# A new hand-written order between the folds of a Fourier layer and the first output tiles of the MLP behind it

## The chip, the cores and the metric

The kernel runs on one core of a Trainium2 chip. A core has a matrix engine (PE in the profile), a vector engine (DVE), a scalar engine (ACT), a general engine (POOL) and a queue that issues most of the transfers (SP). Each engine works through its own instructions in order and waits for the others by semaphores. PE writes only to PSUM, a memory of eight banks, from which DVE and ACT read; POOL works on the main on-chip memory (SBUF) alone. The metric is the time of one execution in microseconds (us), lower is better.

## The reference, cut to what matters

Three layers follow one another on two sequences (b = 0, 1) of 768 tokens with 512 features:

```python
attn = retention(q, k, v, lam)                       # blocks of tokens with a running state
X = np.real(np.fft.fft(np.fft.fft(x, axis=1), axis=2))   # over tokens, then over features
u = x + X
un = (u - mean(u)) / sqrt(var(u) + 1e-6)
u = u + maximum(un @ w_ch1, 0) @ w_ch2               # first MLP, 512 -> 2048 -> 512
xn = (u - mean(u)) / sqrt(var(u) + 1e-6) * g_ln
out = u + maximum(xn @ w_ch1b, 0) @ w_ch2b           # second MLP
```

All of it is computed to nearly float32 accuracy: in the MLPs a float32 operand is split into two 16-bit parts, `hi` and `lo`, and a product is three matmul passes (hi by hi, hi by lo, lo by hi).

## The kernel before

The tokens are handled as twelve tiles of 128: for each sequence three tiles `U[b][0..2]` and three mirrored ones `U[b][3..5]`, since the transform over the tokens is done by its symmetry. MLP work runs in blocks of three tiles (384 tokens); there are four blocks, two a sequence.

Up to the first MLP block everything is a chain for b = 0: retention; the folds (`fold_half`, lines 483 to 499), in which DVE adds and subtracts a tile and its mirror and then folds over the features; the first transform over the tokens (`dft1_part`, `dft1_out`: five groups g of matmuls over three folds m, then ACT copies each group out of PSUM); the second transform over the features, a sine half (`dft2_q`: PE, then two ACT copies into `qs`; `sub_sin`: it is applied to `u` in two additions) and a cosine half (`dft2_p` on PE, `add_cos` on DVE); the norm (`ln_steps`: DVE statistics, two small DVE steps, a power on POOL; `ln_pe_steps`: a small DVE step and the scaling `un` on ACT, four transposes on PE, the copy of the hi part on ACT, the subtraction for the lo part on DVE); and the first output tiles of the MLP (`part`, `mlp_part`: 12 matmuls for one tile of tokens j and one of 16 slices f of the hidden layer). The program does this for f = 0, 1, 2 only, nine parts in all.

Meanwhile weights are converted. `conv_steps` (line 283) makes the two 16-bit halves of a 128x512 weight piece in four steps: ACT expands the upper bits into one of three buffers `top`; DVE shifts the lower bits and combines both (two instructions, lines 294 and 295); ACT rounds to the hi half (308); POOL subtracts for the lo half (310). With `which=None` DVE keeps its middle result in SBUF, with a name of banks ("at", "up") in PSUM. Pieces (1,0,0) to (1,0,3), the first quarter of the first weight matrix, are needed before the first part of the MLP; (2,0,0) and (2,0,1) are the first pieces of the second matrix, and the next quarter of the first is (1,0,4) to (1,0,7).

The order of the stretch is written by hand in the string `ORDER` (line 44). Each word runs the next step of a chain: `k`/`j` are the cosine and sine half of a fold, `d24` the matmuls of fold 2 for group 4, `D3` the copy of group 3, `c0` to `c3` the conversions, `R` the fold of one extra row (ACT then POOL), `q X p P` the second transform of a tile, `b n` the norm, `W27` 27 matmuls whose result is not used, `M12` the part of the MLP for tile 1 and slice 2. PE, DVE, POOL and ACT take these instructions in the order of the string, word by word. In the string of before the steps of the three tiles are mixed; so are the conversions, whose last steps stand among the second transforms:

```python
    chains[f"c{i}"] = lambda i=i: conv_steps(1, 0, i, None if i else "at")
```

Behind the string a planner orders the rest by its own estimate of times: for each step n of the MLP the matmuls up and down and the tasks of a table `bg` (weight conversions, the retention of b = 1, norms). `after(i, task)` (line 973) sets the instructions of a task on one engine behind a gate. The gates are the last POOL power of `ln_steps` ("pool") and the last lo subtraction of `ln_pe_steps` on DVE ("dve"). The mirrored tiles are finished by `dft2_y0` on POOL, behind the gate "pool", and `dft2_y`; conversions (2,0,0) and (2,0,1) stand behind "dve".

Of the kernel before, what the change touches and what calls it, by code (L numbers as in the profile page):

```python
# [15 lines left out]
ALU = mybir.AluOpType  # L16
# [4 lines left out]
B, H, S, D = 2, 8, 768, 64  # L21
# [7 lines left out]
ND = DM // 2 + 1  # L29
# [12 lines left out]
YS = 2.0 ** -15  # L42

ORDER = """
c0 S B1 B0 s s B1 B0 s s O4 B1 B0 O4 c0 I O4 R I O5 O5 O5 O5 c0 c1 c2 W12 k2 j2 k2 k2 d24 d20 d21 j2 j2 d22 d23
k1 k1 k1 d14 d10 d11 j1 j1 j1 d12 d13 c3 j0 j0 j0 d03 k0 k0 k0 d02 c1 D3 R c2 R c0 D2 d04 d01 D4 d00 c3 D1 q0 D0 q0
c1 q2 q2 X0 X0 q1 q1 c2 X1 p0 p1 P0 c1 X1 P1 b0 b1 b0 X2 c3 p2 c2 b0 b1 X2 P2 c3 b0 n0 b1 b2 b1
W27 n0 b2 n1 n0 b2 W6 n1 n0 b2 M00 n2 n1 n2 n2 n1 M01 M12 M11 M10 n2 M22 M20 M02 M21
"""
ONPOOL = "Y1 Y2"  # L50
LD1 = ()
# [1 line left out]
EARLY0, GATEN, B1, SPC, DS, DC, DFO, DD, D1S, D2S, AO, YA, NR, NE, LN1, L1, L2, F01, F02, TL, R1, R2, SE, PR1, LAG, UB, FB, NW, MQ, SPL = 11, 8, 3, 2.0, 2.0, 5, 1.0, 0.5, 0.5, 1.0, "aba", "aa", 2, 0, 2, 2.5, 2.5, 16, 4, 3, 1.5, 2, "dddd_dppp", 0, 3, 3, 13, 11, 1, 3  # L53
# [71 lines left out]
def tile_retention_fourier_mlp(ctx: ExitStack, tc: tile.TileContext, a: dict, out: bass.AP):  # L125
    nc = tc.nc
    pe, act, dve, pool, sp = nc.tensor, nc.scalar, nc.vector, nc.gpsimd, nc.sync
# [18 lines left out]
    def bank(which, name):  # L146
        return banks[which].tile([P, 512], F32, tag=which, name=name)
# [103 lines left out]
    def w_load(kind, m, i, room=None):  # L251
        t = room
        if t is None:
            t = wst.tile([P, 512, 2], I32, tag="ws", name=f"ws{kind}_{m}_{i}")
        staged[kind, m, i] = t
        return sp.dma_start(t.rearrange("p n two -> p (n two)").bitcast(I16)[:, :2047], w_src(kind, m, i).bitcast(I16)[:, 1:2048])
# [6 lines left out]
    def run(steps):  # L263
        for t in steps:
            pass
        return t

    def w_conv(kind, m, i):
        return run(conv_steps(kind, m, i, "at"))
# [13 lines left out]
    def conv_steps(kind, m, i, which=None, into=None):  # L283
        if (kind, m, i) not in staged:
            w_load(kind, m, i)
        raw = staged.pop((kind, m, i))
        top = tops[n_top[0] % 3]
        n_top[0] += 1
        t = wtp.tile([P, 512], F32, tag="wt", name=f"wf{kind}_{m}_{i}")
        ti = t.bitcast(I32)  # L290
        part = ti if which is None else bank(which, f"ps_w{kind}_{m}_{i}").bitcast(I32)
        act.activation(top[:, :, 1], raw.bitcast(BF16)[:, :, 2], AF.Copy, scale=TOPS)  # L292
        yield t
        dve.tensor_scalar(part, raw[:, :, 0], 13, None, op0=ALU.logical_shift_right)  # L294
        dve.tensor_tensor(ti, part, top.rearrange("p n two -> p (n two)").bitcast(I32), op=ALU.bitwise_or)  # L295
        yield t
        if kind == 1:
            g, k = divmod(i, 4)
            if (m, g) not in w1t:
                w1t[m, g] = wpool.tile([P, 2, 4, 512], F16, tag=f"w1_{g}", name=f"w1_{m}_{g}")  # L300
            hi, lo = w1t[m, g][:, 0, k], w1t[m, g][:, 1, k]
        else:
            if into is None:
                into = w2t[m, i] = wpool.tile([P, 2, 512], F16, tag=f"w2_{i}", name=f"w2_{m}_{i}")
            hi, lo = into[:, 0], into[:, 1]
        if kind == 1 and m == 1:
            act.activation(t, t, AF.Copy, scale=gcol[:, k:k + 1])
        act.copy(hi, t)  # L308
        yield t
        (dve if m == 0 and i in (LD1 if kind == 1 else LD2) else pool).tensor_tensor(lo, t, hi, op=ALU.subtract)  # L310
        yield t
# [134 lines left out]
    def attn_s_steps(b, c, bk):  # L446
        new, old = states[c % 2], states[(c - 1) % 2]
        if c > 0:
            dec = stp.tile([P, H // 2 * D], F32, tag="dec", name=f"dec{b}_{c}")
            do, di = (z.rearrange("p (i d) -> p i d", d=D) for z in (dec, old))  # L450
            pool.tensor_tensor(do, di, lc.unsqueeze(2).to_broadcast([P, H // 2, D]), op=ALU.mult)
        yield
        k_ = ks[b, c]
        ps = bank(bk["st"], f"ps_st{b}_{c}")
        for h in range(H):
            (i, e), hc = divmod(h, 2), slice(h * D, (h + 1) * D)
            for n, (x, y) in enumerate(PASS):
                pe.matmul(ps[e * D:(e + 1) * D, i * D:(i + 1) * D], k_[:, x, hc], vs[b, c][:, y, hc],
                          start=n == 0, stop=n == 2)
        yield  # L460
        psv = ps[:, :H // 2 * D]
        if c == 0:
            dve.tensor_copy(new, psv)
        else:
            dve.tensor_tensor(new, psv, dec, op=ALU.add)
        yield
        if b == 0:
            for e in range(2):
                r = slice(e * D, (e + 1) * D)
                act.copy(diag[c % 2][r, :, e * D:(e + 1) * D], new[r].rearrange("p (i d) -> p i d", d=D))  # L470
        yield
# [110 lines left out]

    def sub_sin(b, j, eng=pool):
        qs, x_ = qst[j], U[b][j]
        dve.tensor_tensor(x_[:, :ND], x_[:, :ND], qs, op=ALU.subtract)
        yield
        eng.tensor_tensor(x_[:, ND:], x_[:, ND:], qs[:, 255:0:-1], op=ALU.add)
        yield
# [14 lines left out]
    def dft2_y0(b, j):  # L603
        qs, y_ = qst[j], U[b][3 + j]
        pool.tensor_tensor(y_[:, :ND], y_[:, :ND], qs, op=ALU.add)
        pool.tensor_tensor(y_[:, ND:], y_[:, ND:], qs[:, 255:0:-1], op=ALU.subtract)
# [30 lines left out]
    unT, unt, gate = {}, {}, {}  # L637
# [19 lines left out]
    def ln_n(m, blk, j):  # L657
        u = U[blk // 2][(blk % 2) * 3 + j]
        mv, rs = unt.pop((m, blk, j))
        un = unt[m, blk, j] = f32t(f"un{m}_{blk}_{j}")  # L660
        dve.scalar_tensor_tensor(rs[:, 0:1], mv[:, 0:1], -1.0, rs[:, 1:2], op0=ALU.mult, op1=ALU.mult)
        act.activation(un, u, AF.Identity, bias=rs[:, 0:1], scale=rs[:, 1:2])
# [12 lines left out]
    def ln_pe_steps(m, blk, j, bk):  # L675
        if (m, blk) not in unT:
            unT[m, blk] = untp.tile([P, 2, NK, TB], F16, tag="unT", name=f"unT{m}_{blk}")
        ln_n(m, blk, j)
        yield
        un, t = unt.pop((m, blk, j)), unT[m, blk][:, :, :, j * P:(j + 1) * P]  # L680
        ps = bank(bk["l"], f"ps_l{m}_{blk}_{j}")
        for k in range(NK):
            pe.transpose(ps[:, k * P:(k + 1) * P], un[:, k * P:(k + 1) * P], ident)
        yield
        psv = ps.rearrange("p (k t) -> p k t", k=NK)
        act.copy(t[:, 0], psv)
        yield
        gate["dve"] = dve.tensor_tensor(t[:, 1], psv, t[:, 0], op=ALU.subtract)
        yield
# [238 lines left out]
    def eng(n):  # L928
# [3 lines left out]
    chains = {"s": lambda: attn_s_steps(0, 4, bk0), "O4": lambda: attn_o_steps(0, 4, bk0),  # L932
              "O5": lambda: attn_o_steps(0, 5, bk0), "I": lambda: attn_i_steps(0, 5, bk0), "R": lambda: row_fold(0)}
# [5 lines left out]
    for g in range(5):  # L939
        chains[f"D{g}"] = lambda g=g: dft1_out(0, g, ps1[g])  # L940
    for i in range(NE, 4):
        chains[f"c{i}"] = lambda i=i: conv_steps(1, 0, i, None if i else "at")
    for j in range(3):
        chains[f"q{j}"] = lambda j=j: dft2_q(0, j, bk0)
        chains[f"X{j}"] = lambda j=j: sub_sin(0, j, eng(f"Y{j}"))
        chains[f"b{j}"] = lambda j=j: ln_steps(0, 0, j)
        chains[f"n{j}"] = lambda j=j: ln_pe_steps(0, 0, j, bk0)
# [25 lines left out]
    def after(i, task):  # L973
        with tc.issue_after(gates[i]):
            task()

    gates = {x: g.ins for x, g in gate.items()}
    for j in range(3):
        after("pool", lambda: dft2_y0(0, j))
    after("dve", lambda: [w_conv(2, 0, i) for i in range(2)])  # L980
    for j in range(3):
        dft2_y(0, j, bk0) if YA[0] == "a" else after("dve", lambda: dft2_y(0, j, bk0))

# [21 lines left out]
    for c in range(NCH):  # L1005
        t = B1 + SPC * c
# [3 lines left out]
    n = t + DC + DFO  # L1010
# [25 lines left out]
    n0 = (NB - 1) * NF  # L1036
# [16 lines left out]
    def step(n):  # L1053
        m = n // (NB * NF)
        return m, order[m][n // NF % NB], n % NF
# [3 lines left out]
    for (m, blk), f in fast_from.items():  # L1059
        for kk in range(2):  # L1060
            if m == 0 and blk < 3:
                put(16 * blk + f / 2 + kk - 3, lambda blk=blk, kk=kk: un_sums(0, blk, kk))
            else:
                at = m * NB * NF + order[m].index(blk) * NF
# [4 lines left out]
    for n in range(total + LAG):  # L1069
        rest = None  # L1070
        if n < total:
            m, blk, f = step(n)
            if n >= SPL:
                rest = (mlp_up if f < fast_from.get((m, blk), NF) else mlp_up_fast)(m, blk, f)
        for _, _, task in sorted(bg.pop(n, ()), key=lambda z: z[0]):
            after("dve", task) if n < GATEN else task()
        if n >= LAG:
            mlp_down(*step(n - LAG))
        if rest:
            rest()  # L1080
# [26 lines left out]
```

## Time and profile before

| | us |
|---|---|
| three runs, median (lowest, highest) | 605.07 (604.65, 605.29) |
| the profiled execution | 605.77 |
| its span in the trace | 603.9 |
| last fold on DVE ends | 48.37 |
| last of the nine MLP parts ends | 71.6 |

Times inside the trace are counted from the start of the span. A view that lists instructions merges neighbours of one kind on one engine (x12 is twelve of them) and shows in brackets how long the engine stood idle before them and whose end released it. PE's matmuls overlap one another, so the length of one is more than the step from one to the next.

### The profile page before, as it was taken

The page shows a single profiled execution, that of the slowest core. Times are in us where ns is not written, and L with a number is a line of the kernel's source. Part 1 is how long each engine was busy: PE and PEld are TensorE (multiplying, and loading weights), DVE is VectorE, ACT ScalarE, POOL GpSimd, SP SyncE. Part 2 cuts the span into 40 slices and gives each one's busy share as a digit, 9 for nine tenths or more (in the row PEclk, how much of TensorE's full clock was granted, in tenths as well). Part 3 has the DMA queues.
Part 4 walks back from the last instruction along what each step waited for, and adds up shares of the span by engine and source line. Part 5 has one row for each costly group of instructions (what it writes and reads, how often), then busy time and mean ns, then how long its engine had stood idle before and what let it go on. Part 6 is the DMA issues. An engine that isn't in the chain of part 4 may idle for free.

```text
span 603.9 us, 11882 instructions
## 1 busy us (share of the span) xinstructions
PE 576.7 (95%) x4669; PEld 379.3 (63%) x4669; DVE 416.1 (69%) x905; ACT 262.8 (44%) x530; POOL 280.0 (46%) x294
## 2 busy tenths in 40 slices
PE   6879899999999998999988999999999999999997
PEld 3756646565644554676756677666677777767773
DVE  5998799884794698886697679867544553555333
ACT  3654689654223433453457675753222222221110
POOL 7854789986253666342349665963011200020000
PEclk9899999999999999999998999999999999999999
DMA  8995259962000100443163652510110027102001
GB/s 278 396 400 187 71 176 295 304 205 69 1 1 1 35 19 9 107 130 105 46 194 111 189 162 79 158 27 1 61 28 18 2 79 63 18 1 84 22 2 52
DMA packets 46326, 63.23 MB, mean 105 GB/s; under 512 B 26176, under 2 KB 28350, under 8 KB 46270
## 3 DMA queue, kind: packets, MB, share of 16 engines
q1 hardware_dynamic: 45598, 62.40, 34.4%
q8 instruction: 36, 0.59, 0.4%
q10 hardware_dynamic: 672, 0.08, 0.1%
q14 instruction: 20, 0.16, 0.1%
HBM read 52.23 MB, written 6.29 MB: 97 GB/s over the span
## 4 chain that ended last, share of the span: by engine, by line
PE 62%; DVE 19%; ACT 7%; POOL 6%; issue 4%; DMA 1%; SPq 0%; DVEq 0%; POOLq 0%; ACTq 0%
PE ps_y L848 30%; PE ps L801 22%; PE ps_h L708 4%; DVE wf L295 2%; DVE bst L642 2%; ACT top L292 2%; DVE ps_w L294 2%; DVE tr L761 2%; PE ps_d L518 1%; POOL m L358 1%; POOL w L310 1%; PE ps_s L346 1%; PE ps_i L388 1%; POOL kd L322 1%; ACT w L308 1%
## 5 line engine op out<-in xcount | busy, mean ns | idle before, releaser
L848 PE MATMUL ps_y<-w,h 128*128 128x512 f16 x1152 | 281.9, 380 | 3.5 <-ACT h L833 1.7
L848 PEld LDWEIGHTS <-h 128*128 128x128 f16 x1152 | 109.2, 98 | 102.6 <-ACT h L833 3.8
L801 PEld LDWEIGHTS <-sw 128*128 128x128 f16 x1104 | 94.8, 98 | 23.2 <-issue 7.1
L801 PE MATMUL ps<-th,sw 128*128 128x192 f16 x828 | 92.9, 246 | 5.1 <-DVE s L814 3.6
L801 PEld LDWEIGHTS <-w 128*128 128x128 f16 x828 | 72.6, 99 | 19.1 <-issue 0.8
L310 POOL TENSOR_TENSOR w<-wf,w 128x512 f16<-128x512 f32 x58 | 67.1, 1164 | 36.3 <-ACT w L308 36.2
L833 ACT ACTIVATE h<-ps 128x384 f16<-128x384 f32 x92 | 43.8, 488 | 72.8 <-DVE ps L827 68.4
L708 PE MATMUL ps_h<-unT,w 128*128 128x384 f16 x396 | 73.7, 326 | 1.7 <-DVE h L723 1.6
L801 PE MATMUL ps<-unT,w 128*128 128x192 f16 x552 | 63.6, 248 | 0.0
L834 DVE SCALAR_TENSOR_TENSOR h<-ps,h 128x384 f16<-128x384 f32 x92 | 49.5, 554 | 14.2 <-ACT h L833 12.6
L708 PEld LDWEIGHTS <-w 128*128 128x128 f16 x396 | 36.9, 98 | 29.8 <-issue 3.1
L753 POOL TENSOR_TENSOR sw<-ws,sw 128x512 f16<-128x512 f32 x32 | 37.9, 1197 | 33.9 <-ACT sw L752 33.8
L821 DVE TENSOR_TENSOR t<-ps,s 128x192 f32<-128x192 f32 x46 | 16.3, 353 | 50.3 <-PE ps L801 50.0
L292 ACT ACTIVATE top<-ws 128x512 f16<-128x512 bf16 x57 | 44.2, 777 | 10.4 <-DVE wf L295 10.3
L813 ACT COPY s<-ps 128x192 f32<-128x192 f32 x46 | 14.5, 314 | 73.3 <-PE ps L801 73.3
L671 POOL TENSOR_TENSOR uns<-un,uns 128x512 f16<-128x512 f32 x21 | 24.6, 1171 | 43.6 <-ACT uns L670 43.4
L295 DVE TENSOR_TENSOR wf<-ps_w,top 128x512 int32<-128x512 int32 x61 | 41.3, 681 | 2.4 <-POOL w L310 1.2
L777 POOL TENSOR_TENSOR th<-ts,th 128x384 f16<-128x384 f32 x24 | 22.1, 940 | 43.2 <-ACT th L776 43.2
L308 ACT CAST w<-wf 128x512 f16<-128x512 f32 x58 | 34.9, 609 | 10.3 <-DVE wf L295 10.1
L294 DVE TENSOR_SCALAR ps_w<-ws 128x512 int32<-128x512 int32 x55 | 37.8, 689 | 0.9
L827 DVE TENSOR_TENSOR ps<-ps,s 128x192 f32<-128x192 f32 x46 | 16.6, 361 | 28.6 <-PE ps L801 28.4
L814 DVE TENSOR_TENSOR s<-ps,s 128x192 f32<-128x192 f32 x46 | 16.2, 353 | 27.7 <-ACT s L813 27.6
(161 smaller groups left out, 807.2 us busy)
## 6 DMA issues: line engine op xcount, KB each, us to landing
ws<-in_w SPq DMA_DIRECT2D x25, 511.8 KB, 4.8
ws<-in_w2b SPq DMA_DIRECT2D x16, 511.8 KB, 3.5
ws<-in_w1b SPq DMA_DIRECT2D x16, 511.8 KB, 3.6
kt<-in_kt SPq DMA_DIRECT2D x12, 256.0 KB, 4.1
qt<-in_qt SPq DMA_DIRECT2D x12, 256.0 KB, 5.6
v<-in_v SPq DMA_DIRECT2D x12, 256.0 KB
k<-in_k SPq DMA_DIRECT2D x12, 256.0 KB, 5.9
pre<-in_w SPq DMA_DIRECT2D x4, 511.8 KB
```

The source lines that it names most:

```text
L292: act.activation(top[:, :, 1], raw.bitcast(BF16)[:, :, 2], AF.Copy, scale=TOPS)
L294: dve.tensor_scalar(part, raw[:, :, 0], 13, None, op0=ALU.logical_shift_right)
L295: dve.tensor_tensor(ti, part, top.rearrange("p n two -> p (n two)").bitcast(I32), op=ALU.bitwise_or)
L308: act.copy(hi, t)
L310: (dve if m == 0 and i in (LD1 if kind == 1 else LD2) else pool).tensor_tensor(lo, t, hi, op=ALU.subtract)
L671: pool.tensor_tensor(s_[:, 1], un, s_[:, 0], op=ALU.subtract)
L708: pe.matmul(ps, w[:, i, k, fo:fo + P], x[:, j, k, :], start=n == 0, stop=n == 11)
L753: pool.tensor_tensor(lo, z, hi, op=ALU.subtract)
L801: pe.matmul(ps, lhs, rhs, start=start and n == 0, stop=n == 5, skip_group_check=True)
L833: act.activation(hi, z, AF.Relu)
L834: dve.scalar_tensor_tensor(lo, z, 0.0, hi, op0=ALU.max, op1=ALU.subtract)
L848: pe.matmul(dn[blk][j], h[:, x, j * P:(j + 1) * P], w[:, y], start=f == 0 and n == 0, stop=f == NF - 1 and n == 2)
```

## The change

The string `ORDER` is rewritten from the first conversion's end to the first output tiles. The first steps (ACT) of `c1`, `c2`, `c3` stand right behind the retention, and so do the last of `R` and `c0`. The other steps of `c1` to `c3` follow the folds directly; a further conversion, `a0` (piece (2,0,0), until now the planner's), stands behind them. The transforms and norms go tile by tile: `q0 X0 p0 P0 b0`, then `q2 X2 p1 P1 n0 b1`, and so on. The unused matmuls in the second half go from 27 and 6 to 8. The middle results of `c1` to `c3` and `a0` go to PSUM banks "up" instead of SBUF. In `sub_sin` the first of the two additions runs for b = 0 on the engine of the second, which is POOL for tiles 1 and 2 (`ONPOOL`) and DVE for tile 0. Only (2,0,1) is left behind the gate; that piece and the tasks of the first 8 steps are also set behind a gate on ACT, the hi copy of tile 1.

```diff
-c0 S B1 B0 s s B1 B0 s s O4 B1 B0 O4 c0 I O4 R I O5 O5 O5 O5 c0 c1 c2 W12 k2 j2 k2 k2 d24 d20 d21 j2 j2 d22 d23
-k1 k1 k1 d14 d10 d11 j1 j1 j1 d12 d13 c3 j0 j0 j0 d03 k0 k0 k0 d02 c1 D3 R c2 R c0 D2 d04 d01 D4 d00 c3 D1 q0 D0 q0
-c1 q2 q2 X0 X0 q1 q1 c2 X1 p0 p1 P0 c1 X1 P1 b0 b1 b0 X2 c3 p2 c2 b0 b1 X2 P2 c3 b0 n0 b1 b2 b1
-W27 n0 b2 n1 n0 b2 W6 n1 n0 b2 M00 n2 n1 n2 n2 n1 M01 M12 M11 M10 n2 M22 M20 M02 M21
+c0 S B1 B0 s s B1 B0 s s O4 B1 B0 O4 c0 I O4 R I O5 O5 O5 O5 c1 c2 c3 R c0 R c0 W12 k2 j2 k2 k2 d24 d20 d21 j2 j2 d22 d23
+k1 k1 k1 d14 d10 d11 j1 j1 j1 d12 d13 j0 j0 j0 d03 k0 k0 k0 d02 c1 D3 c1 c2 D2 c2 c1 d04 a0 D4 c3 c3 c2 d01 D1 a0 c3 q0 a0
+q0 X0 X0 a0 d00 D0 q1 q1 X1 X1 p0 P0 b0 b0 b0 b0 q2 q2 X2 X2 p1 P1 n0 b1 b1 b1 b1 p2 P2 n1 W8 n0 n0 n0
+b2 b2 b2 b2 M00 n1 n1 M01 n1 n2 M02 M10 n2 M11 n2 n2 M12 M20 M21 M22
...
-        dve.tensor_tensor(x_[:, :ND], x_[:, :ND], qs, op=ALU.subtract)
+        (dve if b else eng).tensor_tensor(x_[:, :ND], x_[:, :ND], qs, op=ALU.subtract)
...
-        act.copy(t[:, 0], psv)
+        gate["act" if j == 1 else "act2"] = act.copy(t[:, 0], psv)
...
-        chains[f"c{i}"] = lambda i=i: conv_steps(1, 0, i, None if i else "at")
+        chains[f"c{i}"] = lambda i=i: conv_steps(1, 0, i, "up" if i else "at")
+    chains["a0"] = lambda: conv_steps(2, 0, 0, "up")
...
-    after("dve", lambda: [w_conv(2, 0, i) for i in range(2)])
+    after("dve", lambda: after("act", lambda: w_conv(2, 0, 1)))
...
-            after("dve", task) if n < GATEN else task()
+            after("dve", lambda: after("act", task)) if n < GATEN else task()
```

## Rows read from the trace of the kernel before

**Rows 1.** Table by stretch: busy us and instructions of each engine, granted clock, DMA.
```profile
38.99:48.37 9.38, 7.99 (x29) 3.91 (x27) 9.04 (x26) 3.67 (x6) 0.00 (x0) 1.00 0.86 323
48.37:53.31 4.94, 4.94 (x16) 1.43 (x14) 4.62 (x6) 3.40 (x7) 1.78 (x2) 1.00 0.67 185
...
71.62:82.47 10.85, 9.16 (x50) 4.10 (x48) 10.85 (x23) 8.54 (x19) 8.00 (x8) 1.00 0.30 86
82.47:130.00 47.53, 47.40 (x383) 27.35 (x382) 41.59 (x67) 38.92 (x70) 46.90 (x44) 1.00 0.92 281
```

**Rows 2.** Waits of PE, 70 to 130 us; behind the dots 82 us to the end: us, times, longest.
```profile
PE ps_y L848 <- ACT w L308: 1.1, 1, 1.1
PE ps_y L848 <- POOL w L310: 0.6, 1, 0.6
...
PE ps L801 <- DVE s L814: 3.6, 2, 2.2
```

**Rows 3.** Instructions in order of time on DVE: start, length, line, operands, idle before.
```profile
36.14 0.69 DVE L294 TENSOR_SCALAR ps_w<-ws 128x512 int32<-128x512 int32 x1
...
48.08 0.29 DVE L495 TENSOR_TENSOR f<-e 128x129 f32<-128x129 f32 x1
...
49.94 2.24 DVE L295 TENSOR_TENSOR wf<-wf,top 128x512 int32<-128x512 int32 x1
...
52.62 0.69 DVE L295 TENSOR_TENSOR wf<-wf,top 128x512 int32<-128x512 int32 x1
54.84 0.43 DVE L585 TENSOR_TENSOR u<-u,qs 128x257 f32<-128x257 f32 x1 [1.53 <-ACT qs L580]
...
56.83 1.40 DVE L595 SCALAR_TENSOR_TENSOR u<-ps_pq,u 128x256 f32<-128x256 f32 x4
58.15 1.27 DVE L642 BATCH_NORM_STATS2 bst<-u 128x6 f32<-128x512 f32 x2
...
67.55 0.69 DVE L688 TENSOR_TENSOR unT<-ps_l,unT 128x512 f16<-128x512 f32 x1 [0.80 <-ACT unT L686]
```

**Rows 4.** The same for ACT.
```profile
54.36 0.45 ACT L580 ACTIVATE qs<-ps_pq 128x128 f32<-128x128 f32 x2
...
61.65 1.74 ACT L662 ACTIVATE un<-u,rs 128x512 f32<-128x512 f32 x2 [4.64 <-DVE rs L661]
63.29 0.56 ACT L686 CAST unT<-ps_l 128x512 f16<-128x512 f32 x1
```

**Rows 5.** The same for POOL.
```profile
49.85 0.67 POOL L416 TENSOR_TENSOR rhl<-r,rhl 1x257 f16<-1x257 f32 x1 [11.15 <-DVE wf L294]
50.48 1.15 POOL L310 TENSOR_TENSOR w<-wf,w 128x512 f16<-128x512 f32 x1
...
60.82 0.56 POOL L650 TENSOR_TENSOR rs<-rs,neghalf 128x1 f32<-128x1 f32 x1 [0.43 <-DVE rs L648]
...
63.27 0.73 POOL L605 TENSOR_TENSOR u<-u,qs 128x257 f32<-128x257 f32 x1
```

**Rows 6.** The same for PE.
```profile
58.27 3.11 PE L964 MATMUL warm<-expo 128*128 128x256 f16 x27
62.52 0.66 PE L683 MATMUL ps_l<-expo,un 128*128 128x128 f32 x4 [1.14 <-ACT un L662]
...
66.10 5.52 PE L698 MATMUL ps_h<-unT,w 128*128 128x128 f16 x96
```

**Rows 7.** Table by stretch, columns as in rows 1; PE busy first, clock third from the end.
```profile
8.50:12.00 3.50, 2.22 (x39) 1.82 (x40) 2.23 (x5) 2.19 (x4) 2.25 (x3) 1.00 1.05 389
12.00:15.50 3.50, 2.54 (x41) 1.96 (x34) 1.85 (x4) 1.96 (x4) 3.50 (x3) 0.51 1.05 387
...
316.00:319.30 3.30, 0.95 (x10) 0.80 (x10) 2.95 (x8) 3.18 (x8) 2.86 (x5) 1.00 0.34 128
319.30:322.80 3.50, 3.50 (x21) 2.57 (x19) 2.33 (x5) 1.92 (x5) 3.50 (x5) 0.51 0.00 0
...
238.00:239.90 1.90, 0.28 (x3) 0.06 (x1) 0.71 (x2) 1.90 (x5) 1.90 (x3) 1.00 0.00 0
```

## The prediction

> **What bounds the kernel now.** I read the table by stretch first. From 82 to 130 us PE is busy 47.40 of 47.53 us [rows 1], and the waits of PE between 70 and 130 us are two, 1.1 and 0.6 us [rows 2]: behind the first output tiles PE sets the time, so what moves its entry into that stage moves the end, unless PE would have waited there anyway. Ahead of the stage PE is no bound by its amount of work but by a chain through all engines. I then read each engine's instructions in order from 36 to 83 us. The folds keep DVE busy 9.04 of 9.38 us, with POOL at 0.00 [rows 1], and the last ends at 48.37 [rows 3]. Three conversions follow on DVE; it has them done at 53.31 and stands idle 1.53 us for the sine copy of ACT before the first subtraction at 54.84 [rows 3]. The first `un` comes at 61.65, the transposes at 62.52, and from 66.10 PE runs 96 matmuls, eight of the nine parts, without a break until 71.6 [rows 4, 6]. Behind that it waits 0.6 us for POOL's lo half of piece (2,0,0) and 1.1 us for the hi half of a later one [rows 2].
>
> **The change part by part.** The method is to lay the rows' lengths end to end in the new order, each engine in sequence. Laid in the old order they end the ninth part at 71.5; the trace has 71.6.
>
> *Folds.* `R` and `c0` end on POOL now beside the folds: 0.67 and 1.15 us, at about 42.7 to 44.8. The price is seen at 49.94: combining two operands in SBUF took DVE 2.24 us there while POOL ran exactly these two instructions, and 0.69 at 52.62 with POOL idle [rows 3, 5]. So 0 to 1.8 us; I take 1.3, as two blocked instructions lose a little less than POOL's whole lengths. The folds end at 49.7. PE's transform hides most of it: it is busy 7.99 of 9.38 us in the folds and 4.94 of 4.94 in the 5 us behind them [rows 1], so it works off a store of finished folds.
>
> *Four conversions behind the folds.* The middle result in PSUM makes the shift 0.69 instead of about 0.42 long but takes the pair out of POOL's way. A piece is 0.69 and 0.69 less the overlap of neighbours: 1.33 us, four 5.3 us, 49.7 to 55.0 [rows 3]. Before it was three, done at 53.31 with a blockage of 1.55 in them. ACT is in order: `a0`'s hi (taken as 0.6, near the 0.56 of the other 512-wide copy) must go before the sine copies of tile 0 (0.45) [rows 4]. These then end at 56.05 instead of 54.81.
>
> *Tile 0.* `X0` is two DVE instructions of 0.43 with both operands in SBUF. POOL runs `a0`'s lo from 55.8 to 56.9 and then two halves of `X1`, 0.73 each. By the blockage above `X0` ends at 58.1; with no blockage it would be 56.9. The cosine adds (0.75, from 1.40 for four) end at 58.9, the statistics (0.68) and two small steps (0.3, an estimate) at 60.0, the power (0.56) at 60.6 [rows 3, 5]. The small step of `n0`, also two operands in SBUF, waits for half of `X2` until 61.3, and `un` (0.81, from 1.74 for two) ends at 62.15. In the old order it ended at 62.46, so going tile by tile has won back everything and 0.3 more.
>
> *The copies.* The order then puts `n1` ahead of tile 0's hi copy on ACT. `n1` hangs on tile 1's power (62.9) and `P2` (62.9): its `un` runs 63.15 to 63.95. Tile 0's transposes are done at 62.9, but its copy (0.56) ends only at 64.4 and its subtraction at 65.1. Tile 2's statistics are queued behind that subtraction on DVE, so its power ends at 66.7 instead of 63.3, its `un` at 68.4, its transposes at 69.0 (PE does five parts meanwhile), its copy at 69.7 and its subtraction at 70.5 (was 68.24) [rows 3 to 6]. PE has from 68.95 the parts M11 to M22, five of 0.69 (5.52 over eight) [rows 6]: the ninth ends at 72.4 to 72.5. **That is 0.9 us later than before.** If nothing blocks `X0` or `n0` it is 1.2 us better, 0.3 us earlier; if the planner puts other copies between `n1`'s and `n2`'s on ACT, 0.5 us worse.
>
> *Behind the parts.* Piece (2,0,0) is ready, which takes away the wait of 0.6 us [rows 2]. The gate for the other conversions opens 2.2 us later (70.5 against 68.24), with one piece fewer, worth some 1.2 us of POOL and 1.3 of DVE. POOL's six sine additions for the mirrored tiles stand behind tile 2's power and begin at 66.7 instead of 63.27 [rows 5], in front of the lo halves; POOL has 2.85 us of idle in 71.62 to 82.47 [rows 1] that takes this up. I put what is late at 0.3 us (from 0, if the idle takes it all, to 1.0, the excess of the 2.2 us over one piece of 1.2). The extra gate on ACT comes earlier than the one on DVE and costs nothing: the halves of a piece on ACT wait for DVE's anyway. Going from 33 unused matmuls to 8 costs nothing by itself; PE waits there.
>
> *Sum:* 0.9 - 0.6 + 0.3 = 0.6 us on the profiled execution, 605.77 to 606.4. The profiled execution stands 0.7 above the median of the runs; on the median it is 605.07 + 0.6 = **605.7 us**. What a measurement can tell from no change is 0.2%, 1.2 us: no change. With the bounds of each term (-0.3 to 1.4, -0.6, 0 to 1.0) this case spans 604.2 to 606.9.
>
> **A rule that speaks against it.** The TensorE clock stood at 0.51 in 12.00 to 15.50 after PE had shown 2.22 busy of 3.50, and in 319.30 to 322.80 after 0.95 of 3.30; at 238.00 to 239.90, with 0.28 of 1.90 after a full stretch, it stayed at 1.00 [rows 7]. In the new order PE does, between the end of the 8 unused matmuls at 59.8 and 64.4, one set of transposes alone (0.66); before, 27 unused matmuls filled 3.11 us there [rows 6]. The Trainium skill, "TensorE: Matmul & The Clock Gate", section "Part 4: PE-mode transpose", says that a transpose does not count as PE work for the clock as a matmul does. No row here isolates transposes; by that rule the stretch would be idle in the clock's eyes and the lower level (1.2 GHz) likely, by the rows alone it is open.
>
> **The rivals.**
>
> *The clock falls (slower).* Place: 62.5 to 66.5, ahead of and in the first parts; it decides as soon as the granted clock is at the lower level when M00 starts. For it: the two falls above. Against: the stretch at 238, and that a fall depends on where the gap lies. Price: the fall in the rows covers 319.30 to 322.80, and matmuls need twice the time in it, so at most 1.7 us; the parts wait for subtractions in some of that, so 0.7 at the least. Time 605.7 + 0.7 to 1.7 = 606.4 to 607.4, taken as 606.9.
>
> *The conversions were the bound (faster).* If what held PE until 82.47 was the conversion work, not the ninth part, then a piece done early and ACT's queue kept free take away both waits (0.6 and 1.1) [rows 2], and the late parts are hidden: 605.07 - 1.7 = 603.4; with the blockages in the folds and at `X0` milder than taken, 602.9. For it: DVE is busy 10.85 of 10.85 us in 71.62 to 82.47 and POOL 8.00 [rows 1]. Against: its gate opens later by more than one piece.
>
> *The planner redraws the rest.* It orders 82 us to the end anew from other start times. The largest wait of PE there is 3.6 us in two pieces [rows 2]; a redraw may give or take some 2 us, about the longer of the two: 603.7 to 607.7. It lies over the other cases and widens them.
>
> *The change doesn't do what it says:* the reordered stretch ends the parts where they ended, as the chain of copies eats what the tiles win, and nothing else moves: 604.5 to 605.6. This is inside the first case's range.
>
> **How the numbers follow.** The first case with the last 0.41, the clock 0.27, the conversions 0.17, a redraw that decides 0.15 (0.08 up, 0.07 down). Slower by over 0.2% (above 606.3): the clock 0.24, redraw 0.08, the upper end of the first case 0.04: 0.36. Faster (below 603.9): conversions 0.17, redraw 0.07, first case 0.02: 0.26. Within: 0.38. The range goes from 602.7 (conversions with milder blockages) to 608.2 (clock at its full price and a redraw up).
>
> **What would show it.** Right: the last fold ends at 49 to 50 with single fold instructions above 0.8 us; the first sine copy at 55.5 or later; an `X0` instruction above 0.8 us; tile 0's copy behind tile 1's `un`; the ninth part at 72 to 73; no wait for (2,0,0). Wrong: a ninth part before 71; a wait above 1.5 us of PE on a conversion between 73 and 84, which would mean that the late gate costs more than 0.3; a granted clock below 0.9 between 55 and 75, the clock's case; the waits of PE behind 130 us differing by more than 1 us in sum, a redraw.

## The result: 3.3 us slower, and the profile after

Over 22 runs each the changed kernel takes 608.95 us in the median (607.85 to 612.65) and the kernel before 606.08 (604.65 to 609.17). The ratio is 1.0055, with a 95% interval from 1.0042 to 1.0068, or +3.3 us (2.5 to 4.1); the two medians alone are 2.9 us apart. The forecast was +0.6 us and a range that ends at 608.2: the time lies above it. The median of before is 1.0 us higher than that of the three runs from which the forecast started; so the difference, not the time, is what the steps have to answer for.

The spans can't be laid side by side whole. The first fold starts at 38.99 us before and at 41.26 after, though the instructions ahead of it are the same; the clock's falls in the retention differ (0.51 from 12.0 to 18.8 before; 0.50 from 10 to 20 and again from 30.3 to 37.1 after). I therefore measure two lengths inside each trace: the *stretch*, from the start of the first fold to the end of the ninth MLP part, and the *rest*, from there to the end of the span.

| profile | fold start | stretch | rest |
|---|---|---|---|
| before | 38.99 | 32.63 | 532.32 |
| before, second | 38.41 | 32.62 | 532.26 |
| after | 41.26 | 35.28 | 534.32 |
| after, second | 38.46 | 35.11 | 532.90 |
| after, third | 38.51 | 35.12 | 533.07 |

The stretch is 2.5 to 2.65 us longer in each profile of after. The rest of the first of them holds a fall of the clock near 324 us that lasts 6.8 us; in the other two, and in both of before, it lasts 3.4. With equal falls the rest is 0.6 to 0.8 us longer. Together that is 3.1 to 3.4 us, which agrees with the measured difference.

DVE after, in order of time (start, length, line, operation, tiles, idle before): one instruction of the folds, the first sine subtraction, the small step of tile 2's norm.

```profile
45.37 1.76 DVE L494 TENSOR_TENSOR f<-e 128x128 f32<-128x128 f32 x1
...
58.75 1.13 DVE L585 TENSOR_TENSOR u<-u,qs 128x257 f32<-128x257 f32 x1 [1.03 <-ACT qs L580]
...
70.54 0.21 DVE L661 SCALAR_TENSOR_TENSOR rs<-mv,rs 128x1 f32<-128x1 f32 x1
```

POOL after, the same columns: what ran beside the instruction at 45.37.

```profile
44.95 0.92 POOL L416 TENSOR_TENSOR rhl<-r,rhl 1x257 f16<-1x257 f32 x1 [4.00 <-DVE e L489]
45.83 1.14 POOL L310 TENSOR_TENSOR w<-wf,w 128x512 f16<-128x512 f32 x1
```

ACT after: the first sine copies, tile 1's `un`, the hi copies of tiles 0 and 1, three weight expansions, tile 2's `un`.

```profile
58.27 0.45 ACT L580 ACTIVATE qs<-ps_pq 128x128 f32<-128x128 f32 x2
...
65.77 0.81 ACT L662 ACTIVATE un<-u,rs 128x512 f32<-128x512 f32 x1 [1.03 <-DVE rs L661]
67.08 0.59 ACT L686 CAST unT<-ps_l 128x512 f16<-128x512 f32 x1 [0.50 <-PE ps_l L683]
69.31 0.59 ACT L686 CAST unT<-ps_l 128x512 f16<-128x512 f32 x1 [1.64 <-PE ps_l L683]
69.79 0.80 ACT L292 ACTIVATE top<-ws 128x512 f16<-128x512 bf16 x1
70.44 1.38 ACT L292 ACTIVATE top<-pre 128x512 f16<-128x512 bf16 x2
71.69 0.79 ACT L662 ACTIVATE un<-u,rs 128x512 f32<-128x512 f32 x1
```

Table by stretch after, columns as in rows 1 (the clock is third from the end).

```profile
41.26:52.10 10.84, 8.64 (x30) 3.91 (x27) 10.50 (x26) 4.36 (x8) 2.02 (x2) 1.00 0.52 194
...
57.60:61.00 3.40, 2.10 (x15) 1.61 (x13) 2.37 (x4) 1.74 (x7) 3.26 (x4) 1.00 1.01 398
61.00:67.80 6.80, 6.13 (x26) 4.59 (x25) 4.50 (x15) 2.62 (x5) 2.83 (x5) 0.50 0.10 38
```

Waits of PE after, 84 to 250 us (total, times, longest).

```profile
PE ps_h L708 <- DVE h L723: 3.0, 2, 1.6
PE ps_s L346 <- DVE u L432: 1.0, 1, 1.0
PE ps_y L848 <- POOL w L310: 0.7, 1, 0.7
...
```

Four things stand in these rows. The folds last 10.84 us instead of 9.38 [rows 1], with an operation of 0.29 us [rows 3] stretched to 1.76 while POOL works. The clock stands at its lower level (0.50, 1.2 GHz) from 61.00 to 67.80. Tile 2's `un` starts at 71.69, though its last DVE step ended at 70.75: ACT is expanding weights for later pieces. And PE meets waits far behind the stretch: before, the list for 84 to 250 us holds the first of these lines alone, with one wait of 1.6 us. The waits for piece (2,0,0) and for the hi half behind it [rows 2] are gone; from 76 to 84 us the list holds 0.2 us.

### The profile page after: what moved, and what is told of

The parts are those of the page before. It is cut to its first block, busy times and chain, and to the rows that moved or that the text cites. A ratio compares the mean times of both kernels' runs of the same rounds, so it can differ in the third digit from the quotient of the medians.

```text
span 610.9 us, 11827 instructions
## 1 busy us (share of the span) xinstructions
PE 581.4 (95%) x4644; PEld 383.0 (63%) x4644; DVE 417.0 (68%) x903; ACT 263.6 (43%) x530; POOL 281.5 (46%) x296
## 4 chain that ended last, share of the span: by engine, by line
PE 62%; DVE 21%; ACT 7%; POOL 5%; issue 3%; DMA 1%; DVEq 0%; ACTq 0%; POOLq 0%
PE ps_y L848 28%; PE ps L801 21%; PE ps_h L708 4%; DVE wf L295 3%; DVE ps_w L294 3%; PE ps_s L346 2%; ACT top L292 2%; DVE bst L642 2%; PE ps_o L426 1%; PE ps_d L518 1%; DVE tr L761 1%; POOL w L310 1%; DVE h L723 1%; POOL m L358 1%; ACT wf L307 1%
## 5 line engine op out<-in xcount | busy, mean ns | idle before, releaser
L708 PE MATMUL ps_h<-unT,w 128*128 128x384 f16 x396 | 73.0, 326 | 3.1 <-DVE h L723 3.0
L708 PEld LDWEIGHTS <-w 128*128 128x128 f16 x396 | 37.6, 98 | 31.6 <-issue 4.5
L295 DVE TENSOR_TENSOR wf<-ps_w,top 128x512 int32<-128x512 int32 x64 | 43.5, 684 | 2.5 <-POOL w L310 0.6
L294 DVE TENSOR_SCALAR ps_w<-ws 128x512 int32<-128x512 int32 x57 | 39.2, 689 | 0.9
L650 POOL TENSOR_TENSOR rs<-rs,neghalf 128x1 f32<-128x1 f32 x24 | 13.1, 550 | 49.5 <-DVE rs L648 49.2
```

The source lines that it names most:

```text
L708: pe.matmul(ps, w[:, i, k, fo:fo + P], x[:, j, k, :], start=n == 0, stop=n == 11)
```

## Experiments

My theory on seeing this: the longer stretch is the ACT gate, the place of tile 0's hi copy and the clock, each for itself, and the longer rest is the planner's new order. The rival: the four early conversions and the blocked folds hold the stretch, and the clock does nothing that is not hidden. Each ratio is against before, with its 95% interval; stretch and rest come from one profile.

**The gate on ACT, moved to tile 2's copy** (in the changed kernel).

```diff
-        gate["act" if j == 1 else "act2"] = act.copy(t[:, 0], psv)
+        gate["act" if j == 2 else "act2"] = act.copy(t[:, 0], psv)
```

> The changed kernel with its gate on ACT moved from tile 1's hi copy to tile 2's. Gate theory (three weight expansions stand between tile 1's copy and tile 2's scaling on ACT, and delay the ninth part): tile 2's scaling starts 0.9 us earlier, first fold to ninth part falls from 35.3 to 34.3 us, the time by 0.8 to 1.2 us against the changed kernel. Clock theory alone: stays at 35.3. Order theory alone (the new order's own queues cost everything): stays at 35.3.

Measured: 1.0041 [1.0026, 1.0057], stretch 33.77, rest 533.86 (with the long fall near 321). In this profile the clock did not fall in the stretch, so its gain of 1.5 us is gate and clock in one. The next two part them.

**The clock held up**, with the gate as changed, then with both.

```diff
-q0 X0 X0 a0 d00 D0 q1 q1 X1 X1 p0 P0 b0 ... p2 P2 n1 W8 n0 n0 n0
+q0 X0 X0 a0 d00 D0 q1 q1 X1 X1 W10 p0 P0 b0 ... p2 P2 n1 W24 n0 W6 n0 n0
```

> The changed kernel with more unused matmuls, in places where PE waits: 10 before tile 0's cosine half, 24 in place of 8, 6 before the first part. Clock theory: no granted clock of 0.5 between the folds and the ninth part; first fold to ninth part falls from 35.3 to about 34.2, the time by 1.0 to 1.5 us. Gate theory alone and order theory alone: the clock may stay up, but the stretch stays within 0.3 of 35.3, because PE waits for ACT and DVE there.

> Both edits. If clock and gate are separate terms, first fold to ninth part is 33.4 us (the new order's own 0.9 over the 32.6 of before), and the time 0.2 to 1.2 us above before. If the order's own queues are the cause, 34.5 or more. If the rest of the kernel behind the parts was made slower by the planner's new order, the stretch falls to 33.4 but the time stays 2 us or more above before.

Measured: 1.0046 [1.0028, 1.0064] and 1.0038 [1.0025, 1.0051]; stretches 34.68 and 33.77, rests 532.98 and 534.32 (the second again with the long fall). The table by stretch with the clock held:

```profile
61.00:67.80 6.80, 6.42 (x55) 5.36 (x54) 5.28 (x15) 2.55 (x5) 2.97 (x5) 1.00 0.14 56
```

So the fall costs 35.1 to 35.3 less 34.68: 0.4 to 0.6 us. The gate costs 34.68 less 33.77: 0.91 us. The added matmuls cost nothing themselves: with the later gate and no fall, the stretch is 33.77 with them and without. In the timed runs the clock's part does not stand out (1.0046 against 1.0055, intervals that overlap). ACT with both (in order of time) has tile 2's `un` right behind its DVE step, no expansion between:

```profile
64.45 0.56 ACT L686 CAST unT<-ps_l 128x512 f16<-128x512 f32 x1
...
68.11 0.81 ACT L662 ACTIVATE un<-u,rs 128x512 f32<-128x512 f32 x1 [0.87 <-DVE rs L661]
```

**The unused matmuls alone, taken from before.**

```diff
-W27 n0 b2 n1 n0 b2 W6 n1 n0 b2 M00 ...
+W8 n0 b2 n1 n0 b2 n1 n0 b2 M00 ...
```

> The kernel before with 8 unused matmuls in place of 27 and none in place of the 6 (the number of the changed kernel). Clock theory: the clock falls to 0.5 near the first parts in this order too, and first fold to ninth part grows from 32.6 by 0.7 to 1.7. Order theory: the old order keeps PE supplied, so 32.4 to 32.8 and no change of the time.

Measured: 1.0014 [1.0000, 1.0029], stretch 33.23 (+0.6), rest 532.13. The clock stands at 0.50 from 63.90 to 67.30. In the old order, too, those matmuls kept the clock up, and without them the stretch is 0.6 us longer.

**Tile 0's copy ahead of tile 1's `un`**, with the later gate; then the same with the clock held.

```diff
-... p2 P2 n1 W8 n0 n0 n0
+... p2 P2 W8 n0 n0 n1 n0
...
-... X1 X1 p0 P0 b0 ... p2 P2 n1 W8 n0 n0 n0
+... X1 X1 W10 p0 P0 b0 ... p2 P2 W18 n0 n0 n1 n0
```

> The changed kernel with the gate on tile 2's copy and tile 0's transposes and hi copy set ahead of tile 1's scaling in the order. Copy theory (tile 0's copy queues behind tile 1's scaling on ACT, and all tiles behind it): first fold to ninth part falls by 0.9, from 33.8 to 32.9 us. Conversion theory (the fourth conversion alone holds the chain): unchanged, 33.6 to 33.8, the first part only comes earlier. The time follows the stretch: 0.9 us under the kernel with the gate alone.

> The changed kernel with the gate on tile 2's copy, tile 0's copy ahead of tile 1's scaling, and 10 and 18 unused matmuls against a fall of the clock. The run with the copy alone had the clock at 0.5 in the stretch (58.5 to 65.3 us), which hid its effect. Copy theory: with the clock up, first fold to ninth part is 32.9 us. If the copy is not what holds the chain: 33.5 to 33.8. The time: 0.3 to 1.2 us above before in the first case, since the planner's new order behind the parts stays.

Measured: 1.0019 [1.0002, 1.0037] and 1.0026 [1.0007, 1.0044]; stretches 34.13 (the clock fell from 58.5 to 65.3) and 32.79 (it did not), rests 533.08 and 532.97. Against 33.77 the copy's place is worth 0.98 us, where its forecast had 0.9. ACT of the second, with tile 0's copy no longer behind tile 1's `un`, which starts at 63.91:

```profile
63.43 0.58 ACT L686 CAST unT<-ps_l 128x512 f16<-128x512 f32 x1 [0.75 <-PE ps_l L683]
```

In these profiles the clock costs more (34.13 less 32.79: 1.3 us) than in the changed kernel; the timed runs do not show it (1.0019 with the fall's kernel, 1.0026 with the clock held). In the changed kernel tile 0's copy is held up anyway: with a clock of 0.50 by PE (0.50 us in the rows above), at full clock by tile 1's `un`. The two delays lie side by side, and only a part of the fall's price shows.

**The early conversion (2,0,0) given back to the planner**, with the copy first and the later gate; then that without the ACT gate.

```diff
-... c2 c1 d04 a0 D4 c3 c3 c2 d01 D1 a0 c3 q0 a0
-q0 X0 X0 a0 d00 D0 ...
+... c2 c1 d04 D4 c3 c3 c2 d01 D1 c3 q0
+q0 X0 X0 d00 D0 ...
...
-    after("dve", lambda: after("act", lambda: w_conv(2, 0, 1)))
+    after("dve", lambda: after("act", lambda: [w_conv(2, 0, i) for i in range(2)]))
```

> The same, and the fourth conversion given back to the planner behind the gates. Rows laid end to end: the sine copies of tile 0 come 1.3 us earlier and the first subtraction is not blocked by POOL, so first fold to ninth part is 31.1 us, 1.8 below the kernel with the copy alone and 1.5 below before (32.6). Behind the parts PE waits for piece (2,0,0) again, 0.5 to 1.0 us. If the stretch is what counts, the time is 0.5 to 1.5 below before; if the planner's new order behind 84 us costs 1 us in all kernels of this family, 0 to 0.5 above before.

> The changed kernel without the fourth conversion in the order, with tile 0's copy first, and without the extra gate. The same with the gate had the shortest stretch (31.6 us) and the longest time (5 us above before). Theory that the gate on ACT held the conversions back behind the parts: the waits of 1.2 and 1.4 us behind the parts fall below 0.5 in sum each, the stretch stays 31.0 to 31.8, and the time comes out 0 to 1.5 us below before. Theory that the planner's order of the rest is made worse by any shorter stretch without piece (2,0,0): the time stays 2 us or more above before.

Measured: 1.0093 [1.0060, 1.0127] and 1.0082 [1.0051, 1.0112]. The stretches are the shortest of all, 31.58 and 31.78; the rests the longest but one kernel's, 535.16 and 535.86. Against 32.79 the early conversion costs the stretch 1.2 us. PE of the first, the longest of its waits behind the parts:

```profile
243.99 2.11 PE L708 MATMUL ps_h<-unT,w 128*128 128x384 f16 x12 [3.11 <-DVE h L723]
```

A stretch shorter by 1.05 us than before's and a rest longer by 2.8 make +1.8 us; the runs say +5.6. In the first one's profile another 2.3 us lie ahead of the folds (they start at 41.33), in the clock's falls in the retention; and the execution that it shows is the fastest of six (609.89 to 616.77 us). Whether the others fell as long is not known beyond their granted clock, 0.981 in the median against 0.988 before; so what the runs have over +1.8 stays open. Without the ACT gate stretch, rest and time stay nearly the same: the gate was not what made the rest long. What both show is that the stretch alone does not set the time.

**No ACT gate in the changed kernel** (the edit shown), **and the ACT gate alone in before** (its reverse, with the gate on tile 1's copy).

```diff
-    after("dve", lambda: after("act", lambda: w_conv(2, 0, 1)))
+    after("dve", lambda: w_conv(2, 0, 1))
...
-            after("dve", lambda: after("act", task)) if n < GATEN else task()
+            after("dve", task) if n < GATEN else task()
```

> The changed kernel without the extra gate on ACT (the gating of before). Gate theory: the weight expansions find their place earlier or later than between tile 1's copy and tile 2's scaling, first fold to ninth part is 33.8 to 34.0 us (35.3 with the gate, of which the clock had 0.6), the time 0.8 to 1.2 us below the changed kernel, as with the gate on tile 2's copy. Order theory: what is left, 1.5 to 2.5 us above before, stays.

> The kernel before with the extra gate on ACT alone (behind tile 1's hi copy), for both pieces and the tasks of the first 8 steps. Gate theory: three weight expansions come between tile 1's and tile 2's hi copies, tile 2's copy is 1 to 2 us later; PE has other parts to do meanwhile, so first fold to ninth part grows by 0 to 0.7 from 32.6. Redraw theory (the gate makes the planner's order behind 84 us worse): the stretch stays, and the time grows by 1 us or more with PE waits near 120 to 130 and 243 to 248 us.

Measured: 1.0048 [1.0031, 1.0066], stretch 35.17; and 1.0035 [1.0016, 1.0055], stretch 33.31, rest 534.35 (with the long fall). Added to the old order, the gate alone costs 0.7 us in the stretch. Taking it away altogether did not give this back: without it two weight expansions of later pieces stand ahead of the first sine copies (at 53.60 and 55.12), which come 0.8 us later, and so does the first `un`; the clock fell as well. What costs is an expansion in ACT's queue ahead of a tile's copies or `un`. A gate on tile 2's copy keeps them out, a gate on tile 1's copy or none does not.

**The PSUM result alone, in before.**

```diff
-    chains[f"c{i}"] = lambda i=i: conv_steps(1, 0, i, None if i else "at")
+    chains[f"c{i}"] = lambda i=i: conv_steps(1, 0, i, "up" if i else "at")
```

> The kernel before with the conversions' middle results in PSUM, nothing else. Blockage theory: the combining instruction of 2.24 us shrinks to 0.7, DVE is ready earlier but waits longer for the sine copy, so first fold to ninth part stays at 32.6 (32.4 to 32.8) and the time within 0.2%. If the blockage had counted, 1.0 to 1.5 us less.

Measured: 0.9999 [0.9986, 1.0012], stretch 32.75, rest 532.05. The conversion blocked to 2.24 us [rows 3] was hidden. The changed order took away a blockage that cost nothing and made one in the folds.

**The early conversion in the old order**, in DVE's idle time ahead of the first subtraction (with the PSUM result); then with four result buffers instead of three.

```diff
-... c1 D3 R c2 R c0 D2 d04 d01 D4 d00 c3 D1 q0 ...
+... c1 D3 R c2 R c0 D2 a0 d04 d01 D4 d00 c3 a0 D1 q0 ...
...
-... b0 X2 c3 p2 ...
+... b0 X2 c3 a0 p2 ...
...
-... W6 n1 n0 b2 M00 ...
+... W6 n1 n0 b2 a0 M00 ...
...
+    chains["a0"] = lambda: conv_steps(2, 0, 0, "up")
...
-    after("dve", lambda: [w_conv(2, 0, i) for i in range(2)])
+    after("dve", lambda: w_conv(2, 0, 1))
```

> The kernel before with the middle results in PSUM and the fourth conversion alone: its DVE step in the idle 1.5 us ahead of tile 0's first subtraction, its copy behind the other conversions' copies, its POOL step behind the last power. Theory that the fourth conversion is worth its wait behind the parts (1.6 us less stall in the first 20 us there, as in the changed kernel) where it costs the chain nothing: first fold to ninth part 32.6 to 32.9, the time 0.5 to 1.5 us below before. Redraw theory (the planner gives the gain back between 100 and 240 us): time within 0.5 us of before.

> The kernel before with the fourth conversion in the chain, as in the last run of it, and a fourth buffer for the conversions' results: in that run the combining instruction stood idle 3.5 us for POOL to free one of three buffers, and all behind it came 2 us later. Buffer theory: first fold to ninth part is 32.6 to 32.9 us. If the fourth conversion then gives 1.6 us behind the parts and nothing is redrawn, the time is 0.5 to 1.5 us below before. If the planner's new order from 40 us behind the parts on belongs to having piece (2,0,0) early, the rest of the span grows by 0.6 us or more in spite of that, and the time is 0 to 1.5 above before.

Measured: 1.0075 [1.0050, 1.0101], stretch 35.16, rest 536.55; and 0.9986 [0.9968, 1.0005], stretch 33.17, rest 531.93. DVE in the first, then in the second (where the conversion fits):

```profile
56.26 0.69 DVE L295 TENSOR_TENSOR wf<-ps_w,top 128x512 int32<-128x512 int32 x1 [3.51 <-POOL w L310]
```

```profile
53.67 0.69 DVE L295 TENSOR_TENSOR wf<-ps_w,top 128x512 int32<-128x512 int32 x1
```

The first stood still for 3.51 us, since the fourth piece needs one of the three buffers back from POOL; I had not counted buffers. Its rest holds two falls of the clock that before does not have, 3.4 us each, near 127 and 243 us; the second kernel's holds one, near 238. The second is the best version of the study (605.29 us in 12 runs, before 605.95 beside it), but its interval holds 1: not shown faster.

**Second and third profiles** of the kernels as they are.

> A second look at the changed kernel. If the fall of the clock ahead of the first parts belongs to the kernel, the clock is at 0.5 in the stretch again and it takes 35.1 to 35.4 us. If it hangs on where the gap falls, the clock may stay up and the stretch is 34.7.

> A third look at the changed kernel, with the same two outcomes: 35.1 to 35.4 us with the clock down, 34.7 with it up.

> A second look at the kernel before. First fold to ninth part is 32.6 us with the clock up; the rest behind it 532 to 533 us with one fall of the clock near 320 us. A rest that differs by more than 0.7 between the two looks would say that the 0.65 us more of the changed kernels' rest is no difference.

Measured: the rows of the table in the first section. The clock fell in the stretch in 3 of 3 profiles of after (61.0, 58.5 and 59.0 us, 6.8 us each) and in none of 2 of before.

## Why the prediction was wrong, step by step

*The folds* (+1.3, end at 49.7): +1.46, all of it in one instruction of 1.76 us. Right.

*Tile 0.* The first sine copies were put 1.24 us behind those of before and came 1.64 behind (58.27, less the 2.27 by which the folds start later). `X0` was blocked as said: 1.13 us for 0.43. The first `un` ended 0.3 us behind the forecast. Right within half a microsecond.

*The copies* (tile 0's behind tile 1's `un`, 0.9): the mechanism is right and measured 0.98 at full clock.

*The extra gate on ACT, which "comes earlier than the one on DVE and costs nothing: the halves of a piece on ACT wait for DVE's anyway".* **This is the step that failed.** The first step of a conversion on ACT is not a half: it expands weights that lie ready and waits for nothing of DVE's. Once tile 1's copy was out, three expansions stood ahead of tile 2's `un`, whose DVE step ended at 70.75 while ACT took it at 71.69. Price: 0.91 us, which the sum had at nothing. I had allowed 0.5 for other copies between the norms, as an end of the range, without asking what the gate would let through.

*The clock* was the slower rival, at 0.27. It happened, and the clock was still down when the first part started at 67.72; but it began ahead of its place, at 61.0, after 3.40 us in which PE showed 2.10 busy; the first transposes start at 65.98. The Trainium skill says that a transpose does not count as busy for the clock in the way a matmul does ("TensorE: Matmul & The Clock Gate", "Part 4: PE-mode transpose"); transposes that come 5 us later cannot have started this fall, and no run here isolates them. The price was taken from a fall of 3.5 us [rows 7]; this one lasted 6.8, and still it cost 0.4 to 0.6 us and not 0.7 to 1.7, since it lies beside the copy's delay. The sentence that going from 33 unused matmuls to 8 "costs nothing by itself" failed with it, the second step that did.

*Behind the parts* (-0.6 for the wait on (2,0,0), +0.3 for the late gate): +0.6 to 0.8. This is the third step that failed. PE's standstill in the table by stretch (length less busy time), counted from the ninth part's end:

| us behind the ninth part | before | after |
|---|---|---|
| 0 to 20 | 1.69 | 0.31 |
| 20 to 60 | 0.13 | 1.69 |
| 60 to 160 | 0.00 | 0.00 |
| 160 to 200 | 1.78 | 3.63 |

The gain near the parts is 1.4 us and so larger than forecast. Further on it is given back, most of it at a place where PE waits for `h`, the values of the hidden layer, in both kernels. PE before:

```profile
239.84 2.11 PE L708 MATMUL ps_h<-unT,w 128*128 128x384 f16 x12 [1.62 <-DVE h L723]
```

PE after:

```profile
239.64 2.11 PE L708 MATMUL ps_h<-unT,w 128*128 128x384 f16 x12 [1.55 <-DVE h L723]
...
245.46 2.11 PE L708 MATMUL ps_h<-unT,w 128*128 128x384 f16 x12 [1.44 <-DVE h L723]
```

The last step of this kind (L708) starts 168.22 us behind the ninth part before and 168.92 after (168.96 and 168.87 in the other two profiles). These 0.7 us are the difference of the rests. ACT just ahead of it, before and then after:

```profile
237.17 0.93 ACT L776 CAST th<-ts 128x384 f16<-128x384 f32 x2 [3.76 <-DVE ts L767]
```

```profile
242.80 0.92 ACT L776 CAST th<-ts 128x384 f16<-128x384 f32 x2 [2.07 <-DVE ts L767]
```

In both kernels `h` stands in ACT's queue behind these two copies of another task, which wait for DVE, and behind the `un` of a later norm (`h` starts at 238.72 and 244.35). A PE that is ahead only waits longer here, 1.62 us before, 1.55 and 1.44 after; so what it won near the parts does not reach the end. The prediction's first paragraph has this condition ("unless PE would have waited there anyway"), and its term of -0.6 does not apply it. Without the early conversion the same step starts at 171.08 and 171.78, and those rests are 2.8 and 3.5 us longer than before's. That the planner's new order is what moves this place is an inference; no run held its order fixed.

*The sum.* From the changed kernel over the clock held, the gate moved and the copy first, the stretch goes from 35.1 to 35.3 to 34.68, 33.77 and 32.79, where before has 32.63: clock 0.4 to 0.6, gate 0.91, copy 0.98 and 0.2 that are left. These 0.2 are the early conversion's 1.2 less the 1.05 by which the rest of the order is shorter (31.58). With 0.6 to 0.8 behind, that is 3.1 to 3.5 against 3.3 (2.5 to 4.1) measured. The terms of the stretch come from single profiles, and they add up by construction, as each leads to the next kernel. The forecast was 2.7 us short: 0.9 for the gate, 0.4 to 0.6 for the clock, 0.9 to 1.1 behind the parts, and 0.2 for a stretch that without gate and clock is 1.1 us longer than before's and not 0.9.

In the timed runs only gate and copy together stand out: 1.0019 [1.0002, 1.0037] without them, and 1.0026 [1.0007, 1.0044] with the clock held as well, against 1.0055 [1.0042, 1.0068]; the intervals of the last two overlap a little (1.0042 to 1.0044). The rival by which the conversions were the bound is out: the waits it wanted removed are gone, and the kernel is slower.

## What to carry to other kernels

When a gate is added or moved, list what it lets through on that engine's queue and which steps of the critical chain come behind: an instruction that waits for nothing goes first, however little it is needed. A shortened stretch, or a wait removed, counts only when the time behind it is followed too: find the next place where the engine waits for another one anyway, above all where a planner orders what follows. Before a piece of work is moved to an earlier place, count the buffers that it holds and who frees them.

## What the runs showed of the hardware that was not expected

The same instructions do not meet the same clock in each execution: the falls ahead of the folds took the start of the first fold from 38.46 to 41.26 us in three profiles of the changed kernel, and the fall near 320 us lasted 6.8 us in one of them and 3.4 in the others. The whole spans of two single profiles can't be compared more closely than that. And DVE's loss to POOL is not shared out evenly: one instruction of the folds took 1.76 us instead of 0.29 (1.76 and 1.75 in the other two profiles), longer than either of POOL's instructions beside it (0.92 and 1.14), and it ended only when both had ended.
